# A fifth block of exponentials for VectorE in three more groups, and nine more bit pieces on GpSimd

## The chip, the core and the metric

The kernel runs on one core of a Trainium2 chip. A core has five engines that the text names: TensorE (PE, matmuls; PEld is its weight load), ScalarE (ACT, activation functions), VectorE (DVE), GpSimd (POOL) and SyncE (SP, which issues the DMAs here). They share an on-chip memory, the arena, and eight PSUM banks that PE writes and that ACT and DVE read. The metric is device time in microseconds, the median of several executions. One execution was recorded by the hardware profiler; every line of a profile below is from such a record.

## The reference

Input `x` has 2048 rows of 640 columns, in bfloat16. With `xn = layernorm(x)`:

```python
s = attention(xn)          # 32 heads of 20 columns, softmax over all 2048 keys, then @ wo
g = silu(mixer_mlp(xn))    # layernorm, @ w1, gelu, shifted rows, @ w2, residual,
                           # layernorm, @ w3 (1536), gelu, @ w4, residual
out = x + s * g
```

The attention has 32 x 2048 x 2048 exponentials, and they are the bulk of the work beside the matmuls.

## The kernel before

**Groups.** The 32 heads are worked in eight quads of four. For each quad the queries go in four chunks of 512. One quad with one chunk is a group, written (quad, qc), 32 groups in all. In a group the 2048 keys go in 16 key tiles of 128. For one key tile PE makes two score tiles, each of 128 keys by two heads of 512 queries (1024 columns, two PSUM banks). Their exponentials are multiplied with V, and all sums of the group gather in one PSUM bank, the output bank (`PVB`). At the close of the group DVE transposes this bank (line 1697) and takes reciprocals (1699), GpSimd normalises (1705), and DMAs turn the result and store it.

**Two ways to an exponential.** A plain tile goes through ACT (`exp_act`, line 1645). A wide row (`score_rows`, line 1627) does two score tiles in one ACT instruction of 2048 columns. In a *block* (`score_both`) two key tiles are shared out: of their four score tiles two go to ACT and two to DVE. DVE evicts each PSUM bank with a scale and an offset into a 16-bit integer (line 1669, four evictions for a block), whose bits, read as bfloat16, are a straight-line approximation of the exponential. `block_bits` (from line 1542) adds the constants 32, 64 and 96 to these integers: three more bit pieces v = 1, 2, 3 beside the first, v = 0. Each of the four is multiplied with V, or with V times a weight, and summed in the output bank by PE (line 1577). So the two DVE tiles take four sums, and the two ACT tiles of the block one (line 1378).

**Units.** Blocks go in units of one or two. A unit of two has pieces of 4096 columns, a unit of one has pieces of 2048. The tuple `ND[quad][qc]` says how many blocks a group has, and `UNITS` at which positions among the plain tiles they stand. Four blocks are two units of two; a fifth block is a unit of its own. The list `NR` names plain tiles that become wide rows, by their position among the key tiles not in blocks; an entry of 100 + i means position i, and an entry beyond the last position has no effect.

**Who adds the constants.** An added piece is one DVE instruction (line 1565, 16-bit) or, if its key (quad, qc, first block of the unit, v) is in the set `PP`, one GpSimd instruction (line 1563, the same bits taken as 32-bit integers). Before the change, v = 3 of both double units is on GpSimd in every group that has them, and v = 2 of the first unit in seven groups, from (1,3) to (3,1).

**What runs beside it.** The mixer and MLP (first projection with line 1954, second with 1988, third with 2045, fourth with 2074, gelu at 1960 and 2052, silu at 2080 and 2089) is spread over the quads, its matmuls in a helper (`mm_tile`, line 717). Stacks of projected keys and queries (1254) are made ahead of the quads that use them. In quad 7 the output projections run (lines 1804 and 1823), and the last group, (7,3), goes in two halves (`last_half`). There, `keep_busy` gives PE dummy matmuls without a use (lines 1400 and 1405); the pairs in `FLN` say of which of two forms and how many.

**The order.** Nothing is scheduled at run time. The string `TABLE` names, two characters for a task, every task of all engines in one order, with one more character for each choice of PSUM banks or of a buffer. `Planner.follow` reads it, so it fixes the order on each engine; `plan_sync` derives the semaphore waits from the data and buffers. A GpSimd instruction is also made to wait for the fast DVE instruction that stands before it in the table (`held_by`). The bit pieces rotate through three buffers (`SS`), the evicted integers through two (`U`).

Of the kernel before, what the change touches and what calls it, by code (L numbers as in the profile page):

```python
# [472 lines left out]
class Cfg:  # L473
# [5 lines left out]
    def __init__(self, S=2048, D=640, H=32, F=1536):  # L479
# [44 lines left out]
        self.FM = False  # L524
        self.FLN = ()
# [63 lines left out]
        self.FLN = tuple( [(1, 2), (0, 1), (1, 3), (0, 6), (1, 2), (1, 3), (0, 2), (0, 3)])  # L589
# [57 lines left out]
class Gen:  # L647
# [29 lines left out]
    def A(self, name, *key):  # L677
        a = (name,) + key
        self.pl.own(name, a)
        return a  # L680
# [1162 lines left out]
    def finish_qc(self, qc):  # L1843
# [8 lines left out]
        for nl in range(4):  # L1852
# [10 lines left out]
            else:  # L1863
# [7 lines left out]
              reads=resa, writes=[("out", n)], is_dma=True, nbytes=128 * cfg.D * 2, name=f"st_out{n}", stream=f"out{sl}",  # L1871
# [224 lines left out]
    r"$b&c#,$V#6#%#f$@###&#$#9#:#'#-#;#<#=#.$)#>#?#@#A#*#B#C#D#E#(#)$*&d#n$+#F#e#G$,#H$-#2#I#~$2$3#J#K#}$.#g#y$/$0#{$##z#L#M#|#d#+$$$%$4#N$5#r#s$K#k$c$&#O#P"  # L2096
    r"#Q#p#R#o$'$6#t#S#T#U#q#V#W#X#Y#i$P$1#Z#[#u#]$M#^$L#_#v#l$8$d#w&b$}&#`#x$x($y$~%&$%'$7$n#$o$($9$z%(%)$N$:%#$p$q%$$e$O${#a$;#h#b%*$r$Q%%$<$R$E$|$B$D$s)$"
    r"t$u$v$w$A%+(%5#$f#c$F$S$C$?$g&e&&f$h#j&g&l)&m#m%w$$G$i$W$X&n%x$=%y%z%{%6$H%0%$>%:'%;&o&p%<%7%=%,%-$Z$j%1%2%|%>%3&z$$[%4$I%8&h&{&|$T$Y$]$J%?'%@%9%A%B$^"
    r"&}$k&~%~%%C%.&#&$&%&&$U%/'#%I#%S'$_%J&i%N$%K%T$l&q%L%O%P$m%X(&j%Y%M%Z%[%U%]%V%Q%D)%E%F&'&)&&*&+%R%G&,&-$`%^($a%_%`%H%a%b%h$%i%j%k%l%r#%s%t(b%u%c)%d%e%"
    r"f%m(%W%}%n%o%p%q&0'&1&2%g&3&4%v&.&7#&8&9&:&;&5'+$',&k&('-&<#0&>&?'.&/'/'0&6&F&&=&G&H&D)&E&I&J*G$&K*H&*:'*<)*;1&O&&L&P&Q*=*>&R&S*J$*K#&T*@1*B*?'&s&*A('"  # L2100
    r"t&t&u*C&v&w&x*L$&M'*M$&A*E'*F%*P-&N*D&X'*R*O$*N*S&Y*T'*U-*X(X*Q)&@&Z&[&]&^*V'*h$'%$*f''&*I*i#''*g$*W*_*k#'(')'8((Y'*'9':*m&';*l('<'='>*z#*r(*j'1('2*n%"
    r"'?#&_'3'@'4'5*s&*{#&U&V)'A*p('6'7'B'C&W*q$*o+(#'D+%$+)%*e+A,V*['Y#'Z'[&`%&y'K$'L'](W'^&a*|#'M'N'_+&)'O'P*}'+#$*w'*x(*t'E$&C'F&B#/'G'H'I+$$+*#'u'J+C'+E"
    r"+F++&*Z'R$*~'S(]+/$+0#'T'U'V'W+4#+-'+.'#5+,'f$'g'$'h'i'j+''k+H$*u'+J+5%'`$'a*b'b+9#'c+K'd*`'e*v)+:$+S$+V([+B'+D&*y+U'm$+7#+8)'n'o'p'q+i&+j(*c'r+X3+G#+"
    r";*^'s+I)*]+2&+3$+Z1l+t4*d+[+e+1*Y+w+M#+O&+N#+P'*a+v+6+<+k(+y#+{+|+l$'v('w'x+x&'y'z+z%+Q+W#+R(+m+f+_+Y''|#'}'~+g'{+s#,$$+T#(#($+b+L(&$+u$,%(('((+}+=,'#"
    r",(&(%,-',/()(*(++~$,G#+>,#)(,#,H$(-(.,0,2$,5,)(,*%(/+h+n#(0,4,&+^(1,D$(3(2+o#,c(,6,d'(Z+`(^#,E)+],B#(_,C((`(j,X(,7+a+?)*,+'l+p$+c+d+q%,1#,3&,Z,^',`,a#"
    r"7,>,N$'Q,[(a,F'X,?,@,,#,I',O)+r(5$,L$-j(6.}(7,J((8(9,K,;,<,=,M#,8,i$,W',:,.%(:,Y$,9,m#,A,o(,l,k,n6,p-)'-*%(;((<,q,P,]#,Q,_&(=(>(?,e&,h(,j#,s(@,b(A&(B,"
    r"t--%-0-/-9(,f)(C-:$(D(E-'&-(&,g(F-2%-4-5-$(,}(G&,r-%)-1&-3#(H(I-<%-7((J-='(K,w,y,x(L(M(k#,z-+-B$-D-E,~#-8((l(m-#%,R->(-?&(n(o-;(p-G#.7$.8$-&-I-,'-.)(d"
    r"$-J-P(e(N(4(f(c-A$-C%-F#-H((g(P&r(h-@-6,{,u-W#-X&(i+@-R,v-M-Z#)+$)1),)-).)/,|-`'-[)-l$)0)T-a#-V-Y-]#-N)#-n-^%)8(T-Q-q4-b'-K-c&-o(O)(Q-s-p#-r'-O(R-_-t-"
    r"|'-~-S-k$-m)-L,S-U-x#-y%#3/5#/6.~/7.#.%$.(.$(.&(-T-d-v#-w#-e/8/9/:.'.<(/#)-u.=&-{#/$-})(S.+/%/&.5'.@4/'/)&/*.B.C.4/+.6'.L%.M).:'/,/-#4/(/.-z//$/0/1.;#"
    r".D$.k#...l%,T/2/3.E'/4.0.H.G.*.F(.9.?#.J(.>.A$)2#)3.K#./.m#.O$.n&(U/<)4)5.N)6)7.,(q.Z(.].Q#.1.3.-.2.P).U$.R#.T'.V'.I.o.s#.t$.^,U.W.X.a.d.)(r$.Y'.[&(s."  # L2110
    r"S.p$.q((t(u(v(w/;/>#/?/@(V2}#8/A/B.b-f.u(3##.v#4>/C3%3-$3.%.`._.f.r33+3/(30).e3&/D'35363($3+/E38+3*3;3:3'(.w/F3)(/G.g.h/H/I37$32(34#.c.j39$.i/J#/K3J#3"
    r"K&-g.x2~((x/L/M3>/N/O/P(31/Q/R3A3O#3G3$)3@3^&-h3S(3U/S3P%/T/U/V3C3R#)$%3_#)%)&3V3T$3`&3a'-i3X43[3Z3c#3,)'3e))(3b3h&))3j#3d43y#3f3g3=3D3F3i33k3z'3W&3Y("
    r"3B)M3x)N$3M#)O3<3l3H$4$'3N)3?)P/=)Q)R3]3E4-#3I#3{$3r3Q3m/_3o4%$3|)3L)S4''4)#)9$):);4/4($403~#)<.y4,'4*4#%4+)=3q4.()>3p4@#3u/^424?$3}4A&3n4C)x4L'3w4M)3"
    r"s4h$4i'.z)c4B.{4E14G484H3v4&3t4f'4g%444J#464P$414K#4R434S)?(y$(z4D'454F$47({4O#494U$4X4W4Q(/W4u'4N4I4w)(|(}4k#4T$4j)U#)V)[4l#(~)W)X5$#4[4m()Y/Y4Z)Z4V&"
    r"/X(/Z4]4n$/[4^4p&4q(1m4s4t4Y5%%4r'4_4e)](4{#)^)_4}&4v(4x4y4b4|&)`4z4~(5.#50)4a)a)b4`5#*#5)&5*(5+&5F#5G')@()A)B5,5-)C)D.|4:4;5D'5/65&#5E()E4o4d515>5'#5"
# [108 lines left out]
```

## Time and profile before

| | |
|---|---|
| median of 3 runs | 798.77 us (798.69 to 799.2) |
| profiled execution | 798.28 us, its span 796.3 us |
| busy in the span | PE 776.2, ACT 766.1, DVE 730.5, POOL 354.1 us |
| exponentials on ACT, line 1645 | 726 |
| wide exponentials, line 1627 | 13 |
| evictions to integers, line 1669 | 536 |
| bit pieces on DVE, line 1565 | 115 of 4096 columns, 36 of 2048 |
| bit pieces on GpSimd, line 1563 | 68, 3.6 us each |

The span runs from the first to the last instruction. A group of instructions has its busy time, in which overlapping instructions count once, and the mean length of one, in which they count fully. "Idle before" is time in which the engine stood still ahead of these instructions, with what ended it. In the chain of waits each piece of work is followed back to what released it. "PEclk" is the granted TensorE clock as a share of full speed. The running sums of a group close where line 1697 runs: quad 4 closes at 503.9 us, quad 5 at 600.5, quad 6 at 691.5, group (7,0) at 715.2, group (7,2) at 768.6.

### The profile page before, as it was taken

The numbers are of one execution on the slowest core, as the hardware profiler recorded it, in microseconds if no ns is written. First come the engines' busy times: TensorE is split into PE (matmuls) and PEld (weight loads), VectorE is DVE, ScalarE is ACT, GpSimd is POOL, SyncE is SP. The second block draws the span as 40 slices with busy tenths as digits, with TensorE's granted clock in tenths as the row PEclk, the third lists the DMA queues.
The fourth block names the chain that finished last, engine by engine and source line by source line (L and its number), as shares of the span: only waits on it lengthen the run. The fifth ranks groups of instructions, "written<-read, shape, count | busy, mean of one in ns | idle before, by whom it ended". The sixth has DMA issues, their size and how long they took to land.

```text
span 796.3 us, 30009 instructions
## 1 busy us (share of the span) xinstructions
PE 776.2 (97%) x13464; PEld 321.4 (40%) x13464; DVE 730.5 (92%) x1206; ACT 766.1 (96%) x802; POOL 354.1 (44%) x208
## 2 busy tenths in 40 slices
PE   8999999999999999999999999999999999999996
PEld 4433333334444333333434443334333344435454
DVE  7879999999999999999999999999988989899867
ACT  7899999999999999999999999999999999999994
POOL 5355334352456737663443433634232333352453
PEclk9999999999999999999999999999999999999998
DMA  6001463442122222423243131244224112134422
GB/s 208 18 18 52 127 139 80 104 96 59 20 60 53 50 57 63 103 44 86 52 119 74 24 78 26 61 60 83 61 55 117 44 20 70 20 83 119 122 89 78
DMA packets 138671, 57.58 MB, mean 72 GB/s; under 512 B 111040, under 2 KB 133744, under 8 KB 138544
## 3 DMA queue, kind: packets, MB, share of 16 engines
q1 hardware_dynamic: 138544, 55.68, 30.0%
q8 instruction: 105, 1.72, 0.9%
q14 instruction: 22, 0.18, 0.1%
HBM read 34.70 MB, written 10.33 MB: 57 GB/s over the span
## 4 chain that ended last, share of the span: by engine, by line
ACT 51%; PE 43%; DVE 4%; DMA 1%; issue 0%; DVEq 0%
ACT arena L1645 46%; PE psum L717 16%; PE psum L1585 9%; PE psum L1577 6%; PE psum L1378 5%; PE psum L1598 4%; PE psum L890 1%; ACT arena L1627 1%; ACT arena L2052 1%; DVE arena L1669 1%; ACT arena L1960 1%; ACT arena L2080 1%; DMA arena<-in_B_w_dram 1%; DVE arena L1565 1%; PE psum L1064 1%; DVE arena L1823 1%
## 5 line engine op out<-in xcount | busy, mean ns | idle before, releaser
L1645 ACT ACTIVATE arena<-psum 128x1024 bf16<-128x1024 f32 x726 | 676.0, 1037 | 16.3 <-PE psum L1585 10.7
L1669 DVE TENSOR_SCALAR arena<-psum 128x512 uint16<-128x512 f32 x536 | 342.4, 680 | 24.7 <-PE psum L1585 21.0
L1563 POOL TENSOR_TENSOR arena<-arena 128x2048 int32<-128x2048 int32 x68 | 244.6, 3600 | 252.7 <-DVE arena L1565 171.0
L717 PE MATMUL psum<-arena 128*32 128x320 bf16 (+1 forms) x5776 | 324.0, 332 | 0.9 <-DMA arena<-in_B_w_dram 0.3
L1585 PE MATMUL psum<-arena 32*128 32x512 bf16 x1642 | 199.5, 384 | 8.3 <-ACT arena L1645 5.0
L717 PEld LDWEIGHTS psum<-arena 128*32 128x32 bf16 x5776 | 141.2, 96 | 116.5 <-issue 27.0
L1577 PE MATMUL psum<-arena 128*22 128x512 bf16 x2144 | 182.1, 381 | 1.0 <-DVE arena L1697 1.0
L1565 DVE TENSOR_SCALAR arena<-arena 128x4096 uint16<-128x4096 uint16 (+1 forms) x151 | 162.0, 1093 | 1.6 <-PE psum L1577 0.6
L1378 PE MATMUL psum<-arena 128*22 128x512 bf16 x1448 | 138.2, 382 | 0.2
L1585 PEld LDWEIGHTS psum<-arena 32*128 32x128 bf16 x1642 | 55.3, 91 | 179.1 <-ACT arena L1645 104.8
L1598 PE MATMUL psum<-arena 128*32 128x512 bf16 x1368 | 103.9, 380 | 0.2
L1577 PEld LDWEIGHTS psum<-arena 128*22 128x22 bf16 x2144 | 50.0, 91 | 61.7 <-issue 28.0
L1705 POOL TENSOR_TENSOR arena<-arena 128x512 bf16<-128x512 f32 x30 | 40.9, 1364 | 61.1 <-DVE arena L1565 28.0
L1378 PEld LDWEIGHTS psum<-arena 128*22 128x22 bf16 x1448 | 35.2, 90 | 52.1 <-issue 26.8
L1598 PEld LDWEIGHTS psum<-arena 128*32 128x32 bf16 x1368 | 28.4, 95 | 36.9 <-ACT arena L1645 28.7
L2045 DVE CAST arena<-psum 128x512 bf16<-128x512 f32 x48 | 32.7, 683 | 5.0 <-PE psum L717 4.8
L1254 DVE CAST arena<-psum 128x512 bf16<-128x512 f32 x40 | 27.0, 684 | 1.9 <-PE psum L717 1.3
L927 DVE BATCH_NORM_STATS2 arena<-arena 128x6 f32<-128x320 bf16 x54 | 23.7, 475 | 1.4 <-DMA arena<-in_A_x_dram 1.3
L1627 ACT ACTIVATE arena<-psum 128x2048 bf16<-128x2048 f32 x13 | 24.5, 1883 | 0.0
L1697 DVE STREAM_TRANSPOSE arena<-psum 128x512 f32<-128x512 f32 x31 | 21.9, 707 | 1.9 <-PE psum L1577 1.3
L1868 POOL TENSOR_TENSOR arena<-arena 128x640 bf16<-128x640 bf16 x12 | 16.7, 1399 | 14.1 <-DVE arena L1804 5.2
L2052 ACT ACTIVATE arena<-arena 128x6144 bf16<-128x6144 bf16 x4 | 21.1, 5316 | 0.0
(125 smaller groups left out, 354.0 us busy)
## 6 DMA issues: line engine op xcount, KB each, us to landing
arena<-in_B_w_dram SPq DMA_DIRECT2D x48, 160.0 KB, 2.7
arena<-arena SPq DMA_DIRECT2D x124, 32.0 KB, 1.9
arena<-in_B_w_dram SPq DMA_DIRECT2D x4, 960.0 KB, 6.0
arena<-in_A_x_dram SPq DMA_DIRECT2D x8, 320.0 KB, 6.4
arena<-in_A_x_dram SPq DMA_DIRECT2D x16, 160.0 KB, 2.8
out_dram<-arena SPq DMA_DIRECT2D x16, 160.0 KB, 1.8
heads<-arena SPq DMA_DIRECT2D x120, 20.0 KB, 2.0
arena<-keys SPq DMA_DIRECT2D x28, 80.0 KB
```

The source lines that it names most:

```text
L717: ins = e.matmul(pb[32 * c:32 * c + 32, 0:N], lhsT(k, c), rhs(k, c), start=(k == 0), stop=(stop and k == nk - 1), tile_position=(0, 32 * c))
L1378: ins = e.matmul(pb[32 * i:32 * i + 22, 0:512], VA[:, ql, kts[i // 2], i, :], PT[:, slots[i // 2][0].slot, 512 * (i % 2):512 * (i % 2) + 512],
L1563: return e.tensor_tensor(dst.bitcast(I32), U[:, ub, 0:w].bitcast(I32), bass.AP(c.tensor, c.offset, [list(c.ap[0]), [0, w // 2]]), op=ALU.add)
L1565: fa if onp else lambda e, v=v, dst=dst: e.tensor_scalar(dst, U[:, ub, 0:w], EXP_B[v], None, op0=ALU.add),
L1577: ins = e.matmul(pb[32 * i:32 * i + 22, 0:512], wv, dst[:, at:at + 512].bitcast(BF16), start=first, stop=final, tile_position=(0, 32 * i))
L1585: return e.matmul(out, self.KT[32 * i:32 * i + 32, b, 128 * kt:128 * kt + 128], self.QT[32 * i:32 * i + 32, b, 512 * qc:512 * qc + 512], s ...
L1598: ins = e.matmul(out[32 * c:32 * c + 32, :], self.KT[:, b, 128 * kt + 32 * c:128 * kt + 32 * c + 32], self.QM[:, gb, 2 * a + jj, :], start ...
L1627: lambda e: e.activation(self.PT[:, hp[0].slot:hp[0].slot + 2, :], self.psum[:, 512 * h0.slot:512 * h0.slot + 2048].rearrange("p (a b) -> ...
L1645: lambda e: e.activation(self.PT[:, hp.slot, :], self.psum[:, 512 * hs.slot:512 * hs.slot + 1024], AF.Exp, scale=cfg.scale),
L1669: lambda e, k=k, h=h: e.tensor_scalar(U[:, ub, 1024 * at + 512 * k:1024 * at + 512 * k + 512], self.bank(h.slot)[:, :], a_exp, EXP_BIAS, o ...
L1705: return e.tensor_tensor(OnT.rearrange("p (k d a) -> p a k d", k=4, a=4), Ob[:, :].rearrange("p (a k d) -> p a k d", a=4, k=4), in1, op=AL ...
L2045: T("dve", c_dve(512), lambda e, h=h, fc=fc, i=i, G=G: e.tensor_copy(G[:, i, fc, :], self.wbank(h)[:, 0:512]), reads=[wa], writes=at, name ...
```

## The change

`ND` goes from four blocks to five in the groups (5,1), (6,3) and (7,0). `PP` gains piece v = 2 of the first unit in nine groups: (4,0), (4,1), (5,0), (5,1), (5,2), (6,2), (6,3), (7,0), (7,1). The pairs in `FLN` change from 12 dummies of the column form and 10 of the row form to 8 and 12. An option `OST` for the naming of output streams is added and is off, so the stream names stay. The whole of `TABLE` is replaced, from its first entry to its last, since task numbers and the order are new. No function is added.

```diff
+        self.OST = False
...
-        self.FLN = tuple( [(1, 2), (0, 1), (1, 3), (0, 6), (1, 2), (1, 3), (0, 2), (0, 3)])
+        self.ND = ([2, 4, 4, 4], [5, 4, 5, 4], [5, 4, 5, 4], [5, 4, 5, 4], [5, 4, 5, 4], [5, 5, 5, 4], [5, 4, 5, 5], [5, 4, 4, 4])
+        self.PP |= {(q, c, 0, 2) for q, c in ((4, 0), (4, 1), (5, 0), (5, 1), (5, 2), (6, 2), (6, 3), (7, 0), (7, 1))}
+        self.FLN = tuple( [(1, 1), (1, 1), (0, 2), (1, 3), (0, 3), (1, 2), (1, 2), (1, 3), (0, 2), (0, 1)])
...
-              ... stream=f"out{sl}",
+              ... stream=f"out{nl if cfg.OST and split else sl}",
...
 TABLE = (
-    r"$b&c#,$V#6#%#f$@###&#$#9#:#'#-#;#<#=#.$)#>#?#@#A#*#B#C#D#E#(#)$*&d#n$+#F#e#G$,#H$-#2#I#~$2$3#J#K#}$.#g#y$/$0#{$##z#L#M#|#d#+$$$%$4#N$5#r#s$K#k$c$&#O#P"
...
```

Before, `ND` was `([2, 4, 4, 4],) + six times [5, 4, 5, 4] + ([4, 4, 4, 4],)`.

More of the change, by code (lines that the diff above doesn't have):

```diff
@@ L1870, in finish_qc @@
             T("sp", C_SP, lambda e, res=res, n=n: e.dma_start(outv[:, n, :], res),
-              reads=resa, writes=[("out", n)], is_dma=True, nbytes=128 * cfg.D * 2, name=f"st_out{n}", stream=f"out{sl}",
+              reads=resa, writes=[("out", n)], is_dma=True, nbytes=128 * cfg.D * 2, name=f"st_out{n}", stream=f"out{nl if cfg.OST and split else sl}",
               due=None if split else self.at(end, "st"))
@@ L2100 @@
[L2100 to L2103, printed above, removed]
@@ new lines @@
+    r"_$D#`#a#b#c&l$$S$C%+'$F$@$g&e##m%w%$h%x$G%y&z&&{&f&|$T%z%{#j$i$j$H&m&n$[$W$Z$X%5($=$k$>%:)%;%|%<%=&g%>&h%,&i%-%.%0%%1%2$]$J%3&}&~$Y%/#l%6%?)&o&p$I%7%8"
+    r"%@%A%~'%B&#%4%9%D%&$&%%E&&%N(%C$^$l&))$U'#%F%G&j%H&*%I#$_%X&%O%P%Q%R%J%Y$m%Z%K%[%L&q%M%S$%T&+&,(a$`%r%%U%V%m(%W$a&'&-%s%t%u%v%n%h#%i%j%k%o%p%l%c$%}%d%"
+    r"]#2%e%f%g%^%%_%`%q%a%b&.&0&&1&2&3&4&7#&5&8&9&:&;&6&F$&<&>'+%',&=&?&B'-'.'/'0&G&H&D&&E&I&J&(*G#&/&K&L*;$*>*H)*=*:'&O$&P&Q&R*<#&S*?#&@&T*@$*B*A'*J'*K$*C"
+    r"&s$&t&u&v&w*L#*P$*M%(X*O'&x*Q&*D&X$*S*R&M)&N*E#&Y&Z*F#*U'*h$*i'*N&[&]*T#*X*W&A&C'%%'&''(Y*f$'(&^')'**[*V(&_*I*m#*Y&U*g$*n#'8#*k(*r$'9*s)':';'<'1''2'3'"
@@ new lines @@
+    r"4*l%*j'5'='6*z$*{$+A&r&V#&W,V'Y&'Z'[*p(*q'']'^*o'_*|$*e+%#*}#&y't+(''?$'@'A*_'B'C'D+)&'K('L&`)&a'M'N'O'P+&%*w'*t'E$'F+C#+#$'$*x(*`(W#7'G'H+$)+*''I+E*~"
+    r"*Z+-$+F'J+/#'R$'S'T'U'V++''W+,+0$+H'+.#+J+4#+K'f$+5&'g'h'i'j*u&'`(*v''u+''a'k+S#+U'7+B(+V'b'c'd'e#5*b+9&*y+D)+X(+:%+G#+I''>*c*]+[*d+Z+e+2$+t7+v+1+7#+3"
+    r"('m%'n+w'o'p'l+i$'q'r+y7+{'X+8#+|+O#+6*a+j$*^+M$+k'+P&+;+N(+<+='v$'w'x'y'z+R#+x$+b+l#+Q+L'|#'}+T%'~(#($'{+z)(%+_+s#&k+u&+W(+d+c+m(&#(',-$,0+~#(Z+Y'((,"
+    r"##()(*,'(,($+},$#(+,2&,%(+h+`,D(,E),/,4+a(,(,)#,*%,5,8,G&,7,H&,;(-(.(/(0,9+f,1#,B(,&(1(3,C',6(2(T,c&+n(,3(+o#+]+g,++^,d$,X%,Z,:,,(,[+>,.%'s,=,^#+p&,a("
@@ new lines @@
+    r".D#/1.F%/2/3/4.-.E(.H.J$.K'./)2#.?#.A(.G.>.).O$.m(.n$.N)3)4.I)5)6.1/<)1)7.Q#.Z(.P%.].o.,.R$.3.2.T&.V).U3,T.s#,U.~.^.0.X(r$(s.Y'(t(u.t#.W-g(v.p$.`.*.a/"
+    r";.[&/>#/?/@/A/B.q'(w.d.j2}.u(4>3-%/C)[3#*3%3&._.b.r.f3(+3*.v)3/(3.&.S.e.c3+33$35)8/D&-h/E3638/3:30'3'(/F3)$3;/G/H.g/I.h37$32(39(.w.i.x34)/J#/K/L2~#3J$"
+    r"/M/N3>31/P$3G/Q/O3K#3O$3$%/R/S3A/T3S#/U3P)3U3^'3_&3V3@3=3R$3T')$$)%)&-i3`'.y3X#3[3c$3,3Z)')(3a())3b3h'3d#3e$3y$3C3D3F3j%3f3i-3W'3z(3g3Y&3k3l3x3?3H$3I%"
+    r".z)M3B3<3M#3N$4$')N$)O3o3]3E)P)Q)R3r)S3m3Q4%&3{#4-$4/404''3u3L)9$3|$):4)));4(#4*3~$)<)=4,'4##4+)>4.%3q3p4?#424@$3n3}4h'4A'4&4B3s4C4i$3t4E-4L%44414H4M#"
```

172 lines of the change are left out of this document (83 added, 89 removed).

## The prediction

> **What bounds the kernel now.** I read the page first, then the chain of waits, then busy time by stretch, then the groups of instructions.
>
> ```profile
> span 796.3 us, 30009 instructions
> PE 776.2 (97%) x13464; PEld 321.4 (40%) x13464; DVE 730.5 (92%) x1206; ACT 766.1 (96%) x802; POOL 354.1 (44%) x208
> ACT 51%; PE 43%; DVE 4%; DMA 1%; issue 0%; DVEq 0%
> ```
>
> The span is 796.3 us. ScalarE (ACT) is busy for 96% of it, and half of the chain that ended last is ACT. PE looks fuller, but its busy time counts matmuls that overlap, so the chain decides. In order of time the chain reads:
>
> ```profile
> 523.14 21.32 ACT arena L1645 x23
> ...
> 555.09 39.49 ACT arena L1645 x43
> ...
> 641.83 48.67 ACT arena L1645 x53
> 690.50 1.16 ACT arena L2080
> ...
> 708.39 7.34 ACT arena L1645 x8
> 718.43 2.31 PE psum L717 x68
> ```
>
> From 523 to 716 us the pieces it lists are all ACT's: exponentials (line 1645), wide exponentials (1627) and a few tables. After 718 us it passes to PE pieces (line 717, the projections). The stretches are cut where the running sums of quads 4, 5 and 6 and of the first group of quad 7 close; the engines stand in them so:
>
> ```profile
> core 0: us, PE busy (x) PEld busy (x) DVE busy (x) ACT busy (x) POOL busy (x), PEclk, DMA share, GB/s
> 415.00:504.00 89.00, 88.24 (x1582) 37.19 (x1582) 84.95 (x138) 88.63 (x94) 37.12 (x20) 1.00 0.27 57
> 504.00:600.50 96.50, 95.56 (x1508) 35.55 (x1500) 89.17 (x133) 95.51 (x99) 36.54 (x15) 1.00 0.35 67
> 600.50:691.50 91.00, 87.72 (x1528) 36.62 (x1532) 81.62 (x123) 90.97 (x92) 33.47 (x12) 1.00 0.25 56
> 691.50:715.00 23.50, 23.44 (x430) 9.97 (x422) 21.46 (x31) 23.50 (x26) 10.96 (x5) 1.00 0.19 45
> 715.00:768.60 53.60, 52.87 (x1084) 26.46 (x1084) 46.00 (x76) 51.65 (x54) 24.70 (x14) 1.00 0.41 118
> 768.60:796.30 27.70, 20.61 (x532) 13.30 (x524) 19.83 (x34) 16.78 (x18) 8.68 (x7) 0.92 0.25 86
> ```
>
> Between 504 and 715 us (three rows, 211.0 us) ACT is idle for 211.0 - 95.51 - 90.97 - 23.50 = 1.02 us. VectorE (DVE) is busy 89.17 + 81.62 + 21.46 = 192.25 us, 91.1%; GpSimd (POOL) has more than half its time free. So there ACT sets the pace and DVE has 18.75 us to spare. That is just where the change moves work.
>
> **The change part by part.** Durations are busy time divided by count, since neighbours overlap (the mean of one is longer):
>
> ```profile
> L1645 ACT ACTIVATE arena<-psum 128x1024 bf16<-128x1024 f32 x726 | 676.0, 1037 | 16.3 <-PE psum L1585 10.7 <-PE psum L1456 3.2 <-PE psum L1430 0.7
> L1669 DVE TENSOR_SCALAR arena<-psum 128x512 uint16<-128x512 f32 x536 | 342.4, 680 | 24.7 <-PE psum L1585 21.0 <-PE psum L1577 1.3
> L1563 POOL TENSOR_TENSOR arena<-arena 128x2048 int32<-128x2048 int32 x68 | 244.6, 3600 | 252.7 <-DVE arena L1565 171.0 <-DVE arena L1669 17.8 <-PE psum L1577 16.7
> ...
> L1565 DVE TENSOR_SCALAR arena<-arena 128x4096 uint16<-128x4096 uint16 x115 | 138.5, 1221 | 1.5 <-PE psum L1577 0.6
> ...
> L1627 ACT ACTIVATE arena<-psum 128x2048 bf16<-128x2048 f32 x13 | 24.5, 1883 | 0.0
> L1565 DVE TENSOR_SCALAR arena<-arena 128x2048 uint16<-128x2048 uint16 x36 | 23.8, 683 | 0.1
> ```
> ```profile
> L1565 DVE TENSOR_SCALAR arena<-arena x151: 650/1216/1729, 38.2 to 761.7; 128x4096 uint16<-128x4096 uint16 x115, 128x2048 uint16<-128x2048 uint16 x36
> ```
>
> An exponential on ACT costs 676.0/726 = 0.931 us, a wide one 24.5/13 = 1.885; a DVE eviction from PSUM 342.4/536 = 0.639; a DVE bit piece of 4096 columns 138.5/115 = 1.204, one of 2048 columns 23.8/36 = 0.661.
>
> *1. A fifth block in groups (5,1), (6,3) and (7,0).* A block takes two key tiles with four exponentials and gives two of them to DVE: four evictions and three 2048-column pieces. ACT loses six exponentials. In (7,0) six key tiles are left to ACT instead of eight, so the entry 106 of the list of wide rows no longer finds a place: that wide instruction becomes two plain ones before two go. ACT: 726 becomes 722 and 13 becomes 12, so 4 x 0.931 + 1.885 = 5.61 us less, all inside 504 to 715, where ACT is the chain. DVE: 12 x 0.639 + 9 x 0.661 = 13.6 us more, same place. PE: each block has five sums into the output bank where there were two (one for ACT's halves, four for the bit pieces), nine more in all, of four matmuls each.
>
> ```profile
> 642.40 0.61 PE L1577 MATMUL psum<-arena 128*22 128x512 bf16 x8
> 642.84 0.60 PE L1598 MATMUL psum<-arena 128*32 128x512 bf16 x8
> ```
>
> Eight such matmuls pass in 642.84 - 642.40 = 0.44 us, so nine sums are 9 x 0.22 = 2.0 us of PE. PE's idle time in the three rows is 211.0 - 95.56 - 87.72 - 23.44 = 4.28 us, which covers the 2.0; what it costs if that cover is used up is a rival below. The scores of the lost wide row go as two pairs; at most another such 0.44 us, which I put at nothing, covered by the same idle time. No DMA is added or moved between queues: the new option for the output stream is off.
>
> *2. Piece v=2 of the first unit to GpSimd in nine groups.* DVE loses 9 x 1.204 = 10.8 us: two pieces in quad 4 (2.4 us, before 504), six between 504 and 715 (7.2), one in (7,1). GpSimd gains 9 x 3.6 = 32.4 us; in the rows from 415 to 768.6 it is busy 142.8 of 353.6, so it holds them. The sum that reads the piece now waits 3.6 us for it instead of 1.2. How PE bore this for the 68 pieces that GpSimd does already:
>
> ```profile
> who waited for it (us, times):
>   PEld psum L1577: 0.3, 1
> ```
>
> 0.3 us in all, so I take nothing; the upper end is 9 x (3.6 - 1.2) = 21.6 us, if each were awaited bare. Queued behind the added pieces on GpSimd is the normalisation (line 1705), whose result goes by a DMA transpose and a store to DRAM, read again only by the output projections. For quads 4 to 6 nothing near waits for it; for (7,1) it is nearer, at most one piece, 3.6 us; I take nothing, as the GpSimd queue appears nowhere in the chain.
>
> DVE's net between 504 and 715 is 13.6 - 7.2 = +6.4 us; with quad 4, from 415 on, +4.0.
>
> The pieces of line 1565 range from 0.650 to 1.729 us with a median of 1.216, so none of the 151 stood more than about 0.5 us behind a GpSimd instruction of 3.6 us. The Trainium skill ("SBUF — State Buffer", section "Who interferes with whom") says that VectorE's fast two-port modes and GpSimd exclude each other over a shared port pair, and that the later one blocks fully. By that rule an order that starts a piece beside a GpSimd piece would pay up to 3.6 us for it, by the row at most 0.5; the order before evidently keeps them apart, and no run shows yet whether the new one does.
>
> *3. Filler.* The dummy matmuls of the last stretch go from 12 column and 10 row tasks to 8 and 12. They stand where PE waits anyway (20.61 busy of 27.7 us). I take 0; if they all stood in the way, two tasks more or less are under half a microsecond.
>
> *4. The order.* The whole list is new, from its first entry. In work nothing changes before quad 4; the gaps can. Before 504 us the chain's gaps can shrink or grow, and no row of before prices it. The nearest are ACT's idle times in the rows below: 5.8 us over 200 to 350 against 0.4 over 350 to 500. I take 0 and keep 2 us to both sides.
>
> *What is late next.* With 5.61 us of ACT gone, DVE must do 192.25 + 6.4 = 198.65 us in 205.4, 96.7%; if evictions of the feed-forward branch move forward into quad 4, 277.20 + 4.0 = 281.2 in 294.4, 95.5% from 415 on. What a DVE that full does to ACT stands in earlier rows:
>
> ```profile
> 200.00:250.00 50.00, 49.41 (x928) 22.03 (x928) 48.83 (x89) 48.69 (x52) 25.89 (x12) 1.00 0.22 51
> 250.00:300.00 50.00, 49.62 (x826) 19.82 (x818) 48.61 (x83) 47.05 (x51) 30.50 (x15) 1.00 0.23 46
> 300.00:350.00 50.00, 48.59 (x692) 16.69 (x688) 47.32 (x83) 48.50 (x51) 33.47 (x17) 1.00 0.35 78
> 350.00:400.00 50.00, 49.07 (x848) 20.33 (x844) 48.10 (x82) 49.94 (x45) 21.66 (x12) 1.00 0.29 64
> 400.00:450.00 50.00, 49.58 (x856) 20.20 (x852) 47.25 (x71) 49.63 (x53) 19.52 (x13) 1.00 0.35 81
> 450.00:500.00 50.00, 49.69 (x914) 20.95 (x906) 47.86 (x80) 50.00 (x54) 20.71 (x8) 1.00 0.22 43
> ```
>
> From 350 to 500 DVE is busy 143.21 of 150 (95.5%) and ACT idles 0.43 us, 0.3%. From 200 to 350 DVE is at 144.76 (96.5%) and ACT idles 5.76, 3.8%. Over the 294.4 us these are 0.9 and 11.3 us, against 1.39 now: the cost lies between -0.5 and +9.9. The even spread (95.5%) is nearer to the first; I take 1.0%, 2.9 us, so +1.5.
>
> **Sum.** -5.6 (ACT) + 1.5 (ACT waits for a fuller DVE) + 0 for the rest = -4.1 us. The profiled execution took 798.28 us (span 796.3 and 2.0 around it), 0.49 below the median of 798.77. So 794.2 by the profiled execution, **794.7** by the median. 0.2% of it, 1.6 us, is about what a measurement can tell from no change.
>
> **Rivals.**
>
> *DVE becomes the bound (slower).* The new exponentials are paced by evictions on a DVE that has no room, and ACT idles behind it as from 200 to 350 us. Price: 3.8% of 205.4 is 7.8, less 1.02 now, +6.8 - 5.6 = +1.2, if only 504 to 715 suffers; from 415 on +9.9 - 5.6 = +4.3. So 800 to 803. It decides once ACT idles over 6.6 us (3.2%) between 504 and 715. For it: 96.7% without a spread. Against: from 350 to 500 DVE is almost as full and costs nothing; between 200 and 350 the chain also holds the second projection's matmuls (line 717), which fall elsewhere.
>
> *PE takes over.* To end 5.6 us earlier with 2.0 us more work, PE needs 7.6 us of room and shows 4.28. Then the gain is 4.28 - 2.0 = 2.3 us: 796.5. For it: PE busy at 98% there. Against: busy time counts each group's overlapping tail, and weight loads wait for ACT to free PSUM 270 times, so PE is not at its peak:
>
> ```profile
> PEld psum L1585 <- ACT arena L1645: 104.8, 270, 0.8
> ```
>
> *Port exclusion.* If each added GpSimd piece holds up a DVE piece by half its length, 9 x 1.8 = 16.2 us come onto a full DVE, of which the 18.75 spare now less 6.4 and less 5.6 leaves 6.7: +9.5 - 5.6, so some 803. This is the rule of the Trainium skill's page "SBUF — State Buffer" named above. Against it: the maximum of 1.729 us.
>
> *The new order moves the first 500 us or the tail.* 2 to 3 us to either side: 792 or 797.5; it can cancel the gain.
>
> **How the numbers follow.** The forecast has 0.52 (792.5 to 797). DVE as the bound 0.18, nearly all slower, a little within the bound. PE 0.14, mostly faster, some the same. Port 0.04, slower. Order and tail 0.12, half of it still faster. That makes faster 0.65, same 0.14, slower 0.21. The low end is the whole ACT gain with 0.5 from fewer gaps and 1 from the order, 791.7; the high end takes in DVE as the bound up to its middle, 801.
>
> **What would show it.** Right: the ACT groups at 722 and 12; the close of (7,0) 4 us earlier, near 711; ACT still over 98.5% busy up to there, DVE at 95 to 97%. Wrong: ACT idle of more than 3% in that stretch with evictions as releaser; pieces of line 1565 longer than 2 us (port); sums at line 1577 waiting for line 1563; or an ACT stretch as before with a later start of quad 5 (order).

## The result, and the profile after

The changed kernel takes 802.38 us (median of six runs, 800.16 to 803.63), the kernel before 798.73 beside it. The ratio is 1.0039, 95% interval [1.0028, 1.0050]: slower by 3.1 us by the ratio (3.6 by the two medians), where 4.1 us less was forecast. The profiled execution took 800.16 us (span 798.4), 2.2 below its own median. In the changed kernel a line stands 3 further down: 1648 for 1645, 1672 for 1669, 1568 for 1565, 720 for 717. In the kernels of the experiments the shift is 0 to 4.

The page of the changed kernel: span, busy time by engine, the chain by engine.

```profile
span 798.4 us, 29901 instructions
PE 775.9 (97%) x13386; PEld 322.0 (40%) x13386; DVE 733.1 (92%) x1218; ACT 763.4 (96%) x797; POOL 385.4 (48%) x217
PE 49%; ACT 43%; DVE 5%; DMA 1%; SPq 1%; issue 1%; DVEq 0%
```

The counts of instructions changed as forecast. The groups by form (busy, mean ns, idle before):

```profile
L1648 ACT ACTIVATE arena<-psum 128x1024 bf16<-128x1024 f32 x722 | 674.8, 1037 | 20.0 <-PE psum L1588 12.7 <-PE psum L1459 3.2 <-PE psum L1381 1.1
L1672 DVE TENSOR_SCALAR arena<-psum 128x512 uint16<-128x512 f32 x548 | 349.4, 683 | 23.5 <-PE psum L1588 20.1 <-PE psum L1580 0.4 <-PE psum L1601 0.2
L1566 POOL TENSOR_TENSOR arena<-arena 128x2048 int32<-128x2048 int32 x77 | 276.6, 3598 | 254.7 <-DVE arena L1568 153.1 <-PE psum L1580 33.4 <-DVE arena L1672 19.1
```

ACT has 722 exponentials for 726, DVE 548 evictions for 536, GpSimd 77 pieces for 68. ACT's busy time over the whole run fell by 2.7 us (766.1 to 763.4), not by the 5.61 of the sum: an exponential, 1.037 us long in both kernels, now counts 674.8/722 = 0.935 us for 0.931, as less of it overlaps with its neighbours. The chain has gone from ACT (51%) to PE (49%). Two rows of DVE's timeline, first before, then after, show when group (7,0) closes:

```profile
715.20 0.70 DVE L1697 STREAM_TRANSPOSE arena<-psum 128x512 f32<-128x512 f32 x1
```
```profile
716.77 0.71 DVE L1700 STREAM_TRANSPOSE arena<-psum 128x512 f32<-128x512 f32 x1
```

That is 1.57 us later, not 4 earlier. Quad 4 had closed 0.43 us late (503.94 and 504.37 us). The stretch between these two closes, in each kernel from close to close (busy time by engine), before, then after:

```profile
core 0: us, PE busy (x) PEld busy (x) DVE busy (x) ACT busy (x) POOL busy (x), PEclk, DMA share, GB/s
503.94:715.20 211.26, 206.98 (x3460) 82.30 (x3452) 192.51 (x286) 210.25 (x215) 81.16 (x31) 1.00 0.29 60
```
```profile
504.37:716.77 212.40, 207.72 (x3424) 82.59 (x3416) 194.90 (x301) 206.26 (x209) 101.84 (x41) 1.00 0.29 62
```

ACT is busy 4.0 us less and idles 6.1 us instead of 1.0: the time taken from it turned into idle time, most of it (5.3 us) in waits for the score matmuls of PE (line 1588). DVE did not fill (91.8%, not 96.7%). What the chain names between 504 and 716 us, before and after:

```profile
by line: ACT arena L1645 79.9%; ACT arena L2052 5.0%; PE psum L717 3.3%; ACT arena L1627 2.5%; PE psum L1585 2.5%; ACT arena L2080 2.2%; PE psum L1577 1.8%; PE psum L1378 1.1%; ACT L2052 0.6%; ACT L1645 0.6%; PE psum L1598 0.5%; issue 0.0%
```
```profile
by line: ACT arena L1648 36.3%; PE psum L720 17.1%; PE psum L1588 12.2%; PE psum L1580 9.9%; PE psum L1381 6.2%; PE psum L1601 5.3%; ACT arena L2055 5.0%; DMA arena<-in_B_w_dram 1.9%; SPq L2033 1.8%; SPq L1348 1.2%; ACT arena L1630 0.8%; AC
```

ACT's share falls from some 91% to some 43%; PE's five lines rise from 9.2 to 50.7%. New are a load of weights (`in_B_w_dram`) and SyncE's queue, 4.9% together. In order of time, pieces of this chain:

```profile
543.02 1.33 SPq L1348
...
545.67 1.29 SPq L2033
547.00 1.28 SPq L2033
548.32 1.27 SPq L2033
549.64 3.94 DMA arena<-in_B_w_dram
553.67 0.61 PE psum L720 x8
```

PE stands still 1.1 us for that load, by the waits:

```profile
PE psum L720 <- DMA arena<-in_B_w_dram: 1.1, 1, 1.1
```

The span's 2.1 us come so: 0.43 up to the close of quad 4; 1.14 in quads 5 to (7,0); 0.99 in (7,1) and (7,2); -0.46 behind them.

### The profile page after: what moved, and what is told of

Same layout as the page of the kernel before. It is cut to its first block, busy times and chain, and to the rows that moved or that the text cites. A ratio compares the mean times of both kernels' runs of the same rounds, so it can differ in the third digit from the quotient of the medians.

```text
span 798.4 us, 29901 instructions
## 1 busy us (share of the span) xinstructions
PE 775.9 (97%) x13386; PEld 322.0 (40%) x13386; DVE 733.1 (92%) x1218; ACT 763.4 (96%) x797; POOL 385.4 (48%) x217
## 4 chain that ended last, share of the span: by engine, by line
PE 49%; ACT 43%; DVE 5%; DMA 1%; SPq 1%; issue 1%; DVEq 0%
ACT arena L1648 36%; PE psum L720 17%; PE psum L1588 11%; PE psum L1580 8%; PE psum L1381 6%; PE psum L1601 5%; ACT arena L2055 3%; ACT arena L1630 2%; DVE arena L1672 2%; ACT arena L1963 1%; DVE arena L1826 1%; DMA arena<-in_A_x_dram 1%; PE psum L1067 1%; DMA arena<-in_B_w_dram 0%; ACT L1648 0%
## 5 line engine op out<-in xcount | busy, mean ns | idle before, releaser
L1648 ACT ACTIVATE arena<-psum 128x1024 bf16<-128x1024 f32 x722 | 674.8, 1037 | 20.0 <-PE psum L1588 12.7
L1566 POOL TENSOR_TENSOR arena<-arena 128x2048 int32<-128x2048 int32 x77 | 276.6, 3598 | 254.7 <-DVE arena L1568 153.1
L1672 DVE TENSOR_SCALAR arena<-psum 128x512 uint16<-128x512 f32 x548 | 349.4, 683 | 23.5 <-PE psum L1588 20.1
L1588 PE MATMUL psum<-arena 32*128 32x512 bf16 x1676 | 206.0, 384 | 9.2 <-ACT arena L1648 5.0
L720 PEld LDWEIGHTS psum<-arena 128*32 128x32 bf16 x5776 | 141.3, 96 | 115.5 <-issue 26.7
L1568 DVE TENSOR_SCALAR arena<-arena 128x4096 uint16<-128x4096 uint16 (+1 forms) x151 | 158.4, 1067 | 1.6 <-PE psum L1580 0.7
L1588 PEld LDWEIGHTS psum<-arena 32*128 32x128 bf16 x1676 | 57.8, 91 | 186.7 <-ACT arena L1648 99.9
L1601 PE MATMUL psum<-arena 128*32 128x512 bf16 x1232 | 93.7, 381 | 0.4 <-ACT arena L1648 0.2
L1580 PEld LDWEIGHTS psum<-arena 128*22 128x22 bf16 x2192 | 50.4, 91 | 62.0 <-issue 30.1
L1601 PEld LDWEIGHTS psum<-arena 128*32 128x32 bf16 x1232 | 25.1, 95 | 32.3 <-ACT arena L1648 22.4
L1630 ACT ACTIVATE arena<-psum 128x2048 bf16<-128x2048 f32 x12 | 22.7, 1891 | 0.0
L1807 DVE SCALAR_TENSOR_TENSOR arena<-psum,arena 128x320 bf16<-128x320 f32 x32 | 15.2, 488 | 8.0 <-PE psum L720 7.8
```

The costliest lines, as they stand in the source:

```text
L720: ins = e.matmul(pb[32 * c:32 * c + 32, 0:N], lhsT(k, c), rhs(k, c), start=(k == 0), stop=(stop and k == nk - 1), tile_position=(0, 32 * c))
L1566: return e.tensor_tensor(dst.bitcast(I32), U[:, ub, 0:w].bitcast(I32), bass.AP(c.tensor, c.offset, [list(c.ap[0]), [0, w // 2]]), op=ALU.add)
L1568: fa if onp else lambda e, v=v, dst=dst: e.tensor_scalar(dst, U[:, ub, 0:w], EXP_B[v], None, op0=ALU.add),
L1580: ins = e.matmul(pb[32 * i:32 * i + 22, 0:512], wv, dst[:, at:at + 512].bitcast(BF16), start=first, stop=final, tile_position=(0, 32 * i))
L1588: return e.matmul(out, self.KT[32 * i:32 * i + 32, b, 128 * kt:128 * kt + 128], self.QT[32 * i:32 * i + 32, b, 512 * qc:512 * qc + 512], s ...
L1601: ins = e.matmul(out[32 * c:32 * c + 32, :], self.KT[:, b, 128 * kt + 32 * c:128 * kt + 32 * c + 32], self.QM[:, gb, 2 * a + jj, :], start ...
```

## The experiments

Each was timed over five rounds beside the kernel before, which took 798.8 to 799.1 us. A step is the time from one group's close to the next, read in the timeline from the transposes of line 1697.

**Order and GpSimd pieces.** e1 runs the old order up to the close of (4,3) and the new one behind it, with the whole new split; e2 is the reverse, with the old split but for two pieces of quad 4.

```diff
 e1: + ND, PP, FLN as in the change;  TABLE: before's entries to the close of (4,3), then after's
 e2: + self.PP |= {(4, 0, 0, 2), (4, 1, 0, 2)};  TABLE: after's entries to the close of (4,3), then before's
```

> The order of before up to the close of (4,3), then the changed kernel's order; the whole split of work is the changed one. If the loss of 3.6 us comes from the quads with the new split (5 to 7) and their order, this stays at 801 to 803. If it comes from the new order of the first 500 us, this is at 796 to 798.

> The mirror image: the changed kernel's order up to the close of (4,3), with the two pieces of quad 4 on GpSimd, then the order and the split of before. Loss in quads 5 to 7: 798 to 799.5, as before. Loss in the first 500 us: 801 to 803.

e1 took 806.92 us, 1.0097 [1.0084, 1.0111]; e2 802.42, 1.0043 [1.0029, 1.0057]. The seam, where the two orders meet, costs by itself: in e2 the steps of (4,3) and (5,0) grow by 2.2 and 1.7 us, in e1 those of (5,0) and (5,1) by 2.6 and 1.1, and in e1 the two pieces that GpSimd gets in the old order of (4,0) and (4,1) cost 1.7 and 1.6. So the halves do not add up to the whole, and neither total answers the question. The steps away from the seam do: in e2 every step of the old order from (5,1) to (7,0) repeats to 0.02 us; in e1 those of the new order behind (5,2) are those of the changed kernel.

e3 is the kernel before with only the nine pieces on GpSimd; e4 is the changed kernel with them back on DVE.

```diff
 e3: + self.PP |= {(q, c, 0, 2) for q, c in ((4, 0), (4, 1), (5, 0), (5, 1), (5, 2), (6, 2), (6, 3), (7, 0), (7, 1))}
 e4: - the same line, from the changed kernel
```

> The order of before with the nine pieces on GpSimd and nothing else of the change. If pieces on GpSimd come late and hold up the sums (9 x 2.4 us at most, 21.6) or block DVE at the shared port, this is slower by 2 us or more, 801 and above. If they are free, as the forecast has it, 798 to 799, with DVE 10.8 us less busy.

> The changed kernel with the nine pieces back on DVE, in the changed order. If GpSimd's pieces are the cause, it falls to 798 or less. If DVE's room is the cause, 10.8 us more on DVE make it worse than the change, 804 or more. If the order or PE is the cause, it stays near 802.

e3: 810.54 us, 1.0142 [1.0127, 1.0157], some 1.3 us for a piece. e4: 817.96, 1.0231 [1.0216, 1.0246]. From the waits between 400 and 720 us, e3, then e4:

```profile
PE psum L1578 <- POOL arena L1564: 6.2, 7, 1.5
```
```profile
PE psum L1587 <- DVE arena L1671: 5.7, 5, 3.5
PE psum L1579 <- DVE arena L1567: 3.8, 2, 2.0
```

In the old order PE's sums wait for GpSimd; in the new one with the pieces in place none of them does, and without the pieces PE waits for DVE. Behind both losses there is a second wait, which lies inside DVE's instructions and so stands in no list of waits: a fast DVE piece (4096 columns, 16-bit) that starts while GpSimd works goes on until GpSimd's instruction has ended. First DVE and GpSimd in e3, then DVE, GpSimd and PE in e4:

```profile
728.03 4.20 DVE L1566 TENSOR_SCALAR arena<-arena 128x4096 uint16<-128x4096 uint16 x1
723.99 7.16 POOL L1564 TENSOR_TENSOR arena<-arena 128x2048 int32<-128x2048 int32 x2 [2.02 <-DVE arena L1670]
```
```profile
533.01 3.62 DVE L1567 TENSOR_SCALAR arena<-arena 128x4096 uint16<-128x4096 uint16 x1
531.95 3.60 POOL L1565 TENSOR_TENSOR arena<-arena 128x2048 int32<-128x2048 int32 x1 [0.31 <-PE psum L1579]
537.88 0.61 PE L1587 MATMUL psum<-arena 32*128 32x512 bf16 x4 [3.45 <-DVE arena L1671]
```

In e3 GpSimd's two pieces end at 731.15 us; the DVE piece, usually 1.22 us long, ends 1.08 us later. Five DVE pieces of e3 take 2.3 to 4.2 us in this way, and they lie in five of the seven steps that grew by over 1 us. In e4 three take 2.1 to 3.6 us, in the three steps that grew most against the changed kernel (2.5, 5.5 and 3.4 us); the one at 533 us delays the evictions for which PE waits 3.45 us, and from 536.8 us the clock granted to PE is half for 6.8 us. Over all 20 kernels 51 such pieces start with more than 0.1 us of a GpSimd instruction left, and each ends 1.08 to 1.11 us behind that instruction. Evictions from PSUM are not held: in the changed kernel 228 lie inside GpSimd's pieces, with a median of 0.68 us, as outside. So a split needs an order that keeps GpSimd's pieces and the fast DVE pieces apart; how much of e3's and e4's time is this wait and how much the waits of PE listed above was not separated.

**Work taken from or given to one engine.** e5 and e6 change the kernel before, in the groups (5,1), (6,3) and (7,0).

```diff
 e5: + w = 512 if tag in [f"{g}_{k}_{a}" for g in ("5_1", "6_3", "7_0") for k in (0, 1) for a in (0, 1)] else 1024
     + ... e.activation(self.PT[:, hp.slot, 0:w], self.psum[:, 512 * hs.slot:512 * hs.slot + w], ...)
 e6: + for again in range(1 + ((quad, qc) in ((5, 1), (6, 3), (7, 0)) and not first and kts in ((4, 4), (5, 5), (8, 8)))):
```

> Before, order and all else unchanged, but four exponentials on ACT in each of (5,1), (6,3) and (7,0) work on 512 of their 1024 columns: 12 x 0.43 = 5.1 us of ACT left out (half of these scores is old data in the output). It takes ACT's relief alone. The forecast's step (ACT sets the pace from 504 to 715 us, its relief shortens the span one for one): 794. Rival, that PE follows closely behind and ends the gain at 2.3 us or less: 796.5 or more. Rival, that an order made for the old durations gives nothing back: 798.5 to 799.

> Before, but three sums on PE in each of the same three groups are issued twice (those key tiles count double in the output): 9 x 0.22 = 2.0 us of PE more, all else as it is. If PE has room there as the forecast took it: 799, within 0.5. If PE is as tight as ACT: 801.

e5: 799.26 us, 1.0002 [0.9993, 1.0011]. e6: 800.39, 1.0021 [1.0011, 1.0030]. The same stretch, e5 and e6 (before, ACT was busy 210.25 of 211.26 us):

```profile
504.41:715.17 210.76, 206.93 (x3460) 82.44 (x3452) 192.41 (x286) 206.33 (x215) 81.09 (x31) 1.00 0.29 60
```
```profile
504.54:717.36 212.82, 208.52 (x3492) 83.40 (x3484) 192.61 (x286) 211.23 (x215) 81.32 (x31) 1.00 0.28 59
```

In e5 ACT is busy 3.9 us less and the stretch is 0.50 shorter; the rest is idle time of ACT, 4.43 us for 1.01. In e6 2.0 us of added matmuls lengthen the three groups by 0.47, 0.65 and 0.43 us, 1.55 in all, although PE had idle time and ACT was 99.5% busy before. So ACT alone does not set the pace there, and PE cannot take work in for nothing. The likeness of the changed kernel to e5 shows in e7 (the changed kernel without the nine added sums, pieces 1 to 3 of the fifth blocks) and e8 (with twelve exponentials at half width).

```diff
 e7: - ... enumerate([] if acc and v == 0 else blocks)
     + ... enumerate([] if v and blocks[0][0] == 4 and (quad, qc) in ((5, 1), (6, 3), (7, 0)) else blocks)
 e8: + as e5, with k in (4, 5)
```

> The changed kernel and its order, without the nine sums of the fifth blocks' pieces v = 1 to 3 (left out of the output): 2.0 us of PE less. If the added sums are what eats the gain on PE: 799 to 800. If the order's waits are the cause: 802 to 802.5.

> The changed kernel and its order, with four plain exponentials in each of the three groups on half their columns: 5.1 us of ACT less (half of these scores is old data). If ACT still set the pace in the new order: 797. If PE and its waits do: 801.5 to 802.5.

e7: 804.17 us, 1.0072 [1.0060, 1.0085]; e8: 801.87, 1.0040 [1.0028, 1.0053]. Neither relief helps, and e7 lies above both expectations. In e7 the steps of the three groups are those of the changed kernel to 0.2 us; its time grew elsewhere, 2.45 us more than in the changed kernel at (5,2), where PE waited longer for the load, and 1.5 us more at (7,1). The wait, and the 3.4 us behind it (the last figures are clock, DMA share and GB/s):

```profile
PE psum L720 <- DMA arena<-in_B_w_dram: 2.6, 2, 2.2
```
```profile
555.20:558.60 3.40, 3.03 (x28) 0.88 (x32) 0.86 (x2) 1.40 (x2) 3.15 (x1) 0.50 0.00 0
```

Right behind this wait the clock granted to PE is half for 3.4 us, and it is half again from 722.5 to 725.9 us, in (7,1), where PE is busy 26.07 us for 24.58. In the record of the changed kernel, where the wait is 1.1 us, the clock is full up to 793.7 us. So the step of (5,2) holds more than the longer wait; that the wait brought on the lower clock is not shown.

**DVE, and the queue of SyncE.** e11 leaves DVE's nine pieces of the fifth blocks out of the changed kernel. e12 only moves SyncE's entries in its order: the load `ld_w3_3_0` and three DMA transposes go ahead of the load `qm5_3`.

```diff
 e11: + bare = blocks[0][0] == 4 and (quad, qc) in ((5, 1), (6, 3), (7, 0))
      + bare or T("pool" if onp else "dve", ...)
 e12:   SP: ... - qm5_3, ty3_15, ty3_13, ty3_14, ld_w3_3_0
            ... + ld_w3_3_0, ty3_15, ty3_13, ty3_14, qm5_3
```

> The changed kernel with the nine 2048-wide pieces of the three fifth blocks on VectorE left out (their sums read the unshifted integers, so these terms are wrong in the output); VectorE has about 6 us less to do in the three groups. Theory that VectorE's fullness is what cost the time: 797 to 799. Theory that it is TensorE's work and the small waits of the new order: 802, within 1 us of the changed kernel.

> The changed kernel with the load of the last weight slice and three DMA transposes moved ahead of the load in quad 5 that SyncE waits for until 542 us. Theory that TensorE's wait for that slice is part of the loss: the wait of 1.1 us (2.2 in another run) is gone from the trace and the time is 801 to 801.5. Theory that the wait only takes the place of another: 802 to 802.5, as the changed kernel.

e11: 802.78 us, 1.0047 [1.0033, 1.0061], so the load that the fifth blocks put on DVE is not the cause. e12: 800.45, 1.0019 [1.0010, 1.0028], 2.3 below e11 on the same chip, but still slower than the kernel before. SyncE's timeline, in the changed kernel, then in e12:

```profile
542.40 3.22 SPq L1348 DMA_DIRECT2D arena<-arena  x4
545.67 3.93 SPq L2033 DMA_TRANSPOSE arena<-arena  x3
549.64 1.52 SPq L2043 DMA_DIRECT2D arena<-in_B_w_dram  x1
```
```profile
537.16 1.56 SPq L2043 DMA_DIRECT2D arena<-in_B_w_dram  x2
538.77 4.20 SPq L2033 DMA_TRANSPOSE arena<-arena  x3
543.01 2.82 SPq L1348 DMA_DIRECT2D arena<-arena  x4
```

In the new order the load of the weight slice stood behind `qm5_3`, which waits for PE until 542.4 us, and behind three transposes of 1.3 us each. Ahead of them it goes some 12 us earlier and PE's wait is gone. The stretch from quad 5 to (7,0) is then 211.35 us, against 211.26 before.

**Reliefs combined.** All change the kernel before, in the same three groups. The parts: *A*, the twelve half exponentials of e5; *P*, 27 row sums left out (pieces 1 to 3 of blocks 0 to 2); *D*, six 4096-wide DVE pieces left out; *A'*, twelve other exponentials at half width, those that run among the missing sums. In the traces they take less busy time than the expectations say: A 3.9 and A' 3.4 us of ACT, P 3.0 us of PE (e9), D 7.2 us of DVE (e13).

```diff
 P:  + if v and j < 3 and (quad, qc) in ((5, 1), (6, 3), (7, 0)): continue
 D:  + bare = blocks[0][0] == 0 and v < 3 and (quad, qc) in ((5, 1), (6, 3), (7, 0))
 A': + w = 512 if tag in ("5_1_10_0", "5_1_9_0", "5_1_13_1", "5_1_15_1", "6_3_5_1", "6_3_7_1", ...) else 1024
```

> The kernel before, with 27 of its row sums left out (pieces 1 to 3 of blocks 0 to 2 in the groups (5,1), (6,3) and (7,0), so these terms are missing from the output); TensorE has 27 x 0.22 = 5.9 us less to do, and ScalarE and VectorE are as before. Theory that TensorE's list alone sets the pace of quads 5 to 7: 0.8 us of time for each us of work, as the nine added sums cost (1.55 of 2.0), so about 4.6 us less, 794.3. Theory that ScalarE and TensorE are tied there (ScalarE idles 1.0 us of 211): not more than 1 us less, 798. Theory of the prediction (ScalarE alone sets the pace): 799, nothing.

> The kernel before, with the same 27 sums left out and, in the same three groups, twelve exponentials at half their width (the other halves are not computed); TensorE has 5.9 us less and ScalarE 5.1 us less. Theory of the tie (each alone gives nothing, both together give what the smaller is worth): 794 to 795, about 4 to 5 us below before. Theory that TensorE alone sets the pace: the same time as with the 27 sums alone. Theory that neither does (VectorE, or what comes from the order, holds both): 798 or more.

> The kernel before, with six 4096-wide pieces left out on VectorE (pieces 1 and 2 of the first block pair in the groups (5,1), (6,3) and (7,0); their sums read what the slot held before, so these terms are wrong in the output): VectorE has 6 x 1.35 = 8.1 us less to do, ScalarE and TensorE as before. Theory that VectorE alone sets the pace: 792 to 795. Theory of a three-way tie, and theory that the fixed order sets it: 798 to 799.

> The kernel before, with the six pieces of VectorE left out and twelve exponentials of the same groups at half width (VectorE 8.1 us, ScalarE 5.1 us less, TensorE as before). Theory that ScalarE and VectorE are the pair that ties: 794 to 795. Theory of a three-way tie: 797.5 to 799, since TensorE still holds it.

> The kernel before, with the six pieces of VectorE and 27 row sums left out in the same groups (VectorE 8.1 us, TensorE 5.9 us less, ScalarE as before). Theory that TensorE and VectorE are the pair that ties: 793 to 795. Theory of a three-way tie: 797.5 to 799, since ScalarE, idle 1.0 us of 211, still holds it.

> The kernel before, with all three taken from the same groups: six pieces (VectorE 8.1 us less), 27 sums (TensorE 5.9 us less), twelve exponentials at half width (ScalarE 5.1 us less). Theory of a three-way tie: 793.5 to 795, the 4 to 5 us that the least relieved engine is worth. Theory that the fixed order and its hand-overs set the pace: 797 or more, as with ScalarE and TensorE alone (797.8).

> The kernel before, with the 27 sums left out as before and twelve other exponentials of the same three groups at half width, those that run among the missing sums (535-545, 675-687 and 698-706 us); ScalarE 5.1 us and TensorE 5.9 us less, as in the run where they lay apart (1.3 us). Theory that ScalarE and TensorE hold each other locally, over a few us: 3 to 5 us less than before, 794 to 796. Theory that the fixed order or another engine sets it: 797.5 or more, as when they lay apart.

> The kernel before with only those twelve exponentials at half width: ScalarE 5.1 us less in the middle of the three groups, TensorE and VectorE as before. Theory of the prediction (ScalarE is the chain there): 794 to 795. Theory that TensorE's list, only 0 to 4 percent less full there, takes over at once: 798 to 799.

The last column is the change of the time from the close of (4,3) to that of (7,0) in the profiled execution.

| run, parts | us | ratio | close to close |
|---|---|---|---|
| e5, A | 799.26 | 1.0002 [0.9993, 1.0011] | -0.50 |
| e18, A' | 799.01 | 0.9998 [0.9989, 1.0007] | -0.25 |
| e9, P | 798.62 | 0.9995 [0.9986, 1.0004] | -0.08 |
| e13, D | 799.50 | 1.0006 [0.9998, 1.0015] | +0.01 |
| e10, A and P | 797.79 | 0.9986 [0.9978, 0.9995] | -0.83 |
| e14, A and D | 798.37 | 0.9988 [0.9979, 0.9997] | -0.60 |
| e15, P and D | 798.77 | 1.0000 [0.9990, 1.0010] | -0.09 |
| e16, A, P and D | 797.99 | 0.9992 [0.9983, 1.0000] | -0.89 |
| e17, A' and P | 797.73 | 0.9982 [0.9974, 0.9991] | -1.58 |

This refuted more than the prediction. The theory that PE alone sets the pace fell with e9, the tie of ACT and PE alone with e10, the three-way tie as I had put it (all three together give 4 to 5 us) with e16. In e16 the missing work lay apart, though: the halved exponentials ran at 526 to 529, 664 to 669 and 697 to 701 us, the missing pieces at 533 to 536, 673 to 677 and 693 to 694, the missing sums at 535 to 547, 675 to 691 and 697 to 715. e17, where the halved exponentials and missing sums meet, gave the most, but 1.6 us and not 3 to 5. Its rows, the stretch and pieces of its chain:

```profile
505.12:714.80 209.68, 203.03 (x3334) 80.17 (x3326) 192.21 (x286) 206.43 (x215) 81.20 (x31) 1.00 0.29 60
```
```profile
537.55 1.09 DVE arena L1565
538.67 1.29 DVE arena L1672 x2
539.95 2.34 DVE arena L1565 x2
...
669.86 3.04 DVE arena L1672 x5
672.92 1.23 DVE arena L1565
...
680.57 1.03 ACT arena L1648
681.64 0.45 PE psum L1587 x4
682.12 1.95 ACT arena L1648 x2
684.11 0.61 PE psum L1600 x8
...
696.84 3.62 DVE arena L1672 x6
```

Where both ACT and PE have less to do, the chain goes to DVE within a few us, and elsewhere to and fro between ACT and PE. So three engines run close behind one another in their fixed lists, and time taken out of one, or two, turns into waits for the next. Stays open: whether all three relieved at the same moments would give all that the smallest relief is worth, or whether the hand-overs of the fixed order hold something back even then. That was not run.

## Why the prediction was wrong

**Part 1, the failed step:** "4 x 0.931 + 1.885 = 5.61 us less, all inside 504 to 715, where ACT is the chain", and from it one for one. ACT did lose 4.0 us of busy time there, and none of it reached the end: with the load moved ahead in SyncE's queue (e12) the stretch takes 211.35 us, as before. e5 and e18 take about as much from ACT (3.9 and 3.4 us of busy time) with nothing else changed and gain nothing that the medians show (0.50 and 0.25 us by the steps). ACT was the chain by a hair. What the chain names in e5 between 504 and 716 us:

```profile
by line: ACT arena L1646 59.1%; PE psum L717 8.6%; PE psum L1585 7.7%; PE psum L1577 6.1%; ACT arena L2053 5.0%; PE psum L1378 4.0%; PE psum L1598 3.7%; ACT arena L1627 2.6%; ACT arena L2081 1.6%; ACT L2053 0.6%; ACT L1646 0.6%; DVE arena L
```

PE's five lines have 30.1% for 9.2, in a stretch only 0.5 us shorter. An idle time of 1.02 us said that ACT was full, not that it was alone.

The same part covered the nine sums, 2.0 us, with 4.28 us of PE's idle time. e6 shows that this cover does not exist: 1.55 of 2.0 us show. In the changed kernel PE's busy time rose by only 0.7 us over the stretch, and leaving the sums out (e7) changes nothing in their groups, so they are not where its loss comes from.

**Part 2,** nothing for the GpSimd pieces: right in the new order, in whose waits no PE line names GpSimd; in the old order, not made for them, a piece costs some 1.3 us of the 2.4 that were the upper end (e3). But the upper end counted only the sums that wait for a piece, and e3 loses time on DVE as well. The fast DVE pieces, in the changed kernel and in e3:

```profile
L1568 DVE TENSOR_SCALAR arena<-arena x151: 680/1218/1816, 38.9 to 763.8; 128x4096 uint16<-128x4096 uint16 x106, 128x2048 uint16<-128x2048 uint16 x45
```
```profile
L1566 DVE TENSOR_SCALAR arena<-arena x142: 650/1216/4196, 38.3 to 773.7; 128x4096 uint16<-128x4096 uint16 x106, 128x2048 uint16<-128x2048 uint16 x36
```

In the changed kernel the maximum is 1.816 us for 1.729 before and the median unchanged: four DVE pieces are held, by 0.2 to 0.7 us and 1.7 us in all, where before it was one by 0.6. The Trainium skill ("SBUF — State Buffer", "Who interferes with whom") has the later of two such instructions wait for the other. Where DVE comes second the traces agree: each of these pieces, and e3's of 4.196 us, ends 1.08 us behind the GpSimd instruction during which it starts. Where GpSimd comes second no run here shows it, since the table makes a GpSimd piece wait for the fast DVE instruction ahead of it.

**Part 3,** the filler at nothing, was not tried alone; behind (7,2) the changed kernel is 0.46 us faster.

**Part 4,** the order at 0 with 2 us to both sides: mis-sized, and all of the loss that could be placed is here. About half of it is the load behind SyncE's queue: 802.38 us with it, 800.45 without, 1.6 us by the ratios (two comparisons, each beside the kernel before, whose intervals touch; e11, which keeps the wait, lies clear of e12). The wait for it differs, 1.1 us in the record of the changed kernel, 2.2 in that of e7 and 0.2 in that of e8, and the step of (5,2) by -0.35 to +3.18 us between kernels with this order. So it may explain part of the spread from 800.2 to 803.6 us as well; of these six executions only the fastest has a record, so that is not shown. The prediction looked for DMAs added or moved between queues, and not at what a load stands behind in its own queue. At least 1.0 us more are the steps of (7,1) and (7,2), in every kernel with the new order; their cause was not separated, and e15, with the old order there, has 1.2 us more in them too.

**What is late next,** 1.5 us for a fuller DVE: the work over the run is as costed (+2.6 us busy for 13.6 - 10.8), but the new order spreads it, and between quad 5 and (7,0) DVE gained 2.4 us, not 6.4. ACT's new idle time is not its doing (e11).

**Rivals.** "DVE becomes the bound" gave 800 to 803 and holds the measured time by luck: ACT's idle time, 6.1 us, stays under the 6.6 that it asked for, and ACT waits for PE's score matmuls, not for evictions. "PE takes over" named the new chain rightly, but left a gain of 2.3 us, since it still let ACT's time count until PE's idle time was used up; and PE alone is not the bound either (e9). "Port exclusion" names a wait that these traces do show, up to 3.1 us for a piece in e3; in the changed kernel, whose order keeps the two apart, it is 1.7 us of DVE's time in all. "The new order moves the first 500 us or the tail" had the cause of the loss, in quad 5 and 7 rather than there.

## What to carry to other kernels

A chain of waits that names one engine for 90% of a stretch does not say how far behind the next one is. Where another engine is busy 98% and a third 91% beside it and all follow lists fixed in advance, price a relief of the first at what the others leave, perhaps nothing, and take work out of one alone to see. When an order is made anew, look up for each load what stands ahead of it in its queue and what that waits for: moving one load and three transposes gave back about half of what the change had lost. And when work goes from DVE to GpSimd, compare the lengths of the fast DVE instructions and not only the waits: here a piece that met a GpSimd instruction grew from 1.2 to as much as 4.2 us.

## What was not expected of the hardware

Steps repeat far more closely than the medians suggest. In the thirteen kernels with the old order behind quad 4, edits or none, the step of (5,3), 29.77 us, repeats to about 0.02. In the kernels that begin with the old order, what differs from one execution to the next arises by the close of (0,0) (0.5 us earlier to 1.5 later than in the kernel before) and in the steps of (0,2), (1,0) and (4,0), up to 0.9 us, and once (e15) in those of (7,1) and (7,2), 1.2 us; in those with the new order also at (5,2), at the load, and in e7 at (7,1), where the clock falls. Steps between closes therefore tell apart edits of 0.2 us that the medians, some 1 us wide, cannot.
